# Dense layers in two passes over the blocks, float64 weights converted in two portions, and low parts of the expert weights on VectorE

## The chip, the cores and the metric

The kernel runs on one core of one Trainium2 chip. The metric is the device time of one execution in microseconds; less is better. 787.5 us is the median of three runs (787.34 to 787.77).

## What is computed

Three stages follow each other; `x` of one is the input of the next.

```python
# 1. linear attention: B, H, S, D = 4, 8, 768, 48
cur = einsum('bhd,bhe->bhde', u * k_t, v_t)
y_t = einsum('bhd,bhde->bhe', r_t, state + cur)
state = w * state + einsum('bhd,bhe->bhde', k_t, v_t)
# 2. experts: 3072 tokens of 384, 8 experts of width 1024, top 1
y[mask] = gate_w * (relu(x[mask] @ w1[e]) @ w2[e]);  x = x + y
# 3. dense layers, width 2048
h = x @ w_in
out = (h * tanh(log1p(exp(min(h, 20))))) @ w_out
```

`w_in` and `w_out` arrive in float64. The chip is given their 64-bit words and makes float32 values of them.

## The kernel before

**Numbers in two parts.** Matrix products of stages 2 and 3 run in a 32-bit matmul format that keeps fewer bits than float32. Each operand is held as a high part (a ScalarE copy into that format) and a low part (the operand minus its high part), and a product is three matmuls: high by high, low by high, high by low.

**Attention** (lines 673 to 760): 24 units `u` (6 chunks of 128 tokens by 4 pairs of heads). `load_unit(u + 3)` loads two tiles of a later unit through SP's queue; three buffers hold the `at` tiles, so that a load waits until `cv_unit` (L409) has read the buffer's last content. Per unit VectorE scales (L351, L352), masks (L392, two), adds (L463) and multiplies (L409); GpSimd multiplies twice (L361, L371). Results go to `xd` in memory. Routing into slots of 256 tokens per expert follows.

**Weights.** `wb` holds 32 expert bundles of 128x1536 float32, each with 256 columns of `w1` and the matching rows of `w2`. `bundle_load` (L106) loads one, `bundle_hi` (L118, ScalarE, L121) and `bundle_lo` (L123, L125, VectorE or GpSimd) split it into a ring of five slots. Bundles 0 to 2 are split in quarters during attention (`WU`, L659), their low parts on GpSimd; bundle 3 before the expert loop, the other 28 in the loop, low parts in turn on VectorE and GpSimd (L892). `w64` holds 8 dense bundles of 128x1536 float64. `conv` (L165) turns a piece of 384 columns into float32: a ScalarE absolute value (L178), five VectorE instructions (L180, L183, L187, L189, L191) and a GpSimd addition (L194). There are 32 pieces. Six are done in attention, two steps a unit (`conv_step(2)`, L686), 26 in the expert loop and just ahead of it, two together every second iteration (`conv_most`, L899).

**Experts** (L875 to 900): 32 iterations `i`, one bundle each. TensorE does `gemm1(i + 1)` (18 matmuls of 256 columns, L826) and `gemm2(i)` (12 of 384 columns, L848). VectorE forms the low part of the hidden values (L836), of the next expert's tokens (L810) and the expert's output (L855). The split of bundle `i + 4` and the conversion follow on each engine's queue in the order in which they are written; nothing reorders them.

**Dense layers** (L1194 to 1213): 6 blocks of 512 tokens, block by block, 16 items `f` of 128 hidden columns each: 96 items. `ff1(i + 2)` (9 matmuls of 512 columns, L1101) fills one of four PSUM banks `h`. ScalarE and VectorE turn it into `g` and its two parts (`act_in`, `act_inv`, `act_g`, `act_split`; five VectorE and five ScalarE instructions of 128x512). `ff2(i - 2)` (9 matmuls, L1162) adds into three PSUM banks `o`, which a block's last item empties (L1168 ScalarE twice, L1170 VectorE once). The next block's transposes (L1081 to 1083) lie in items 6, 8 and 10. For the last 16 items `ff1` runs three items ahead instead of two (`LA`). The split of the dense bundles is done at the end of the expert stage and at the start of the dense stage, on VectorE (L911, L1177) and GpSimd (L1178 to 1190, L1212).

Of the kernel before, what the change touches and what calls it, by code (L numbers as in the profile page):

```python
# [34 lines left out]
NLO_A = 2  # L35
HC = 384
W_LO, W_HI = 0.8, 1.25
E20 = 485165195.40979
F64_TINY = 3.4332275390625e-05
# [3 lines left out]
def kernel(  # L43
# [24 lines left out]
    pc = pa.enter_context(tc.tile_pool(name="pc", bufs=1))  # L68
    rs_ = ExitStack()
    ws = rs_.enter_context(tc.tile_pool(name="ws", bufs=3, side="right"))  # L70
    wc_ = rs_.enter_context(tc.tile_pool(name="wc", bufs=2, side="right"))
# [58 lines left out]
    def dense_tile(q, dt=F32):  # L130
        pool = pools["wa"] if q < NLO_A else pools["wb"]
        return pool.tile([128, 1536], dt, tag=f"d{q}", name=f"d{q}")

    def dense_f32(q):
        if q not in dense_t:
            dense_t[q] = dense_tile(q)
        return dense_t[q]

    def dense_hi(q, lo=0, hi=1536):
        n = q + (q > 0)  # L140
        if lo == 0:
            h = ring_tile((NE * NB1 - NW_A - NW_B + n // 2) % (NW_A + NW_B), "hl"[n % 2])
            wtile[NE * NB1 + q] = [h, None]
        A.activation(out=wtile[NE * NB1 + q][0][:, lo:hi], in_=dense_f32(q)[:, lo:hi], func=ACTF.Copy)

    def dense_lo(q, eng, lo=0, hi=1536):
        w = wtile[NE * NB1 + q]
        if lo == 0:
            w[1] = dense_tile(q - 1, F32R) if q else ring_tile((NE * NB1 - NW_A - NW_B) % (NW_A + NW_B), "l")
        eng.tensor_tensor(out=w[1][:, lo:hi], in0=dense_f32(q)[:, lo:hi], in1=w[0].bitcast(F32)[:, lo:hi], op=ALU.subtract)  # L150

    cv_raw = {}

    def conv_load():
# [5 lines left out]
        more = "mp1" in pools and n % 3 == 2  # L160
        t = (pools["mp1"] if more else wc_).tile([128, HC], I64, tag="r64", name="r64")
        nc.sync.dma_start(out=t, in_=w64[q, :, HC * s:HC * s + HC])
        cv_raw[n] = t

    def conv():  # L165

        n = cnt["conv"]
        if n >= NCV:
            return
        cnt["conv"] += 1  # L170
        q, s = divmod(n, NHC)
        if not wide:
            nc.sync.dma_start(out=dense_f32(q)[:, HC * s:HC * s + HC], in_=w64[q, :, HC * s:HC * s + HC])
            return
        raw = cv_raw.pop(n).bitcast(I32).rearrange("p (n two) -> p n two", two=2)
        lo, hi = raw[:, :, 0], raw[:, :, 1]
        mag = wc_.tile([128, HC], F32, tag="mag", name="mag")
        A.activation(out=mag, in_=hi.bitcast(F32), func=ACTF.Abs)  # L178
        a = wc_.tile([128, HC], I32, tag="cva", name="cva")
        V.tensor_scalar(out=a, in0=hi, scalar1=3, scalar2=0x3FFFFFF8,  # L180
                        op0=ALU.logical_shift_left, op1=ALU.bitwise_and)
        yield
        V.scalar_tensor_tensor(out=a, in0=hi, scalar=-0x40000000, in1=a, op0=ALU.bitwise_and, op1=ALU.bitwise_or)  # L183
        yield
        b = wc_.tile([128, HC], F32, tag="cvb", name="cvb")

        V.scalar_tensor_tensor(out=b, in0=mag, scalar=F64_TINY, in1=a.bitcast(F32), op0=ALU.is_ge, op1=ALU.mult)  # L187
        yield
        V.tensor_scalar(out=a, in0=b.bitcast(I32), scalar1=-0x800000, scalar2=None, op0=ALU.bitwise_and)  # L189
        yield  # L190
        V.scalar_tensor_tensor(out=mag, in0=lo.bitcast(U32), scalar=2.0 ** -52, in1=a.bitcast(F32),  # L191
                               op0=ALU.mult, op1=ALU.mult)
        yield
        G.tensor_tensor(out=dense_f32(q)[:, HC * s:HC * s + HC], in0=b, in1=mag, op=ALU.add)  # L194
        yield

    cheld = []

    def conv_most(n):

        new = [conv() for _ in range(n)]
        for c in new:
            next(c, None)
        for _ in range(4):
            for c in new:
                next(c, None)
        cheld.extend(new)

    def conv_sum():
        while cheld:  # L210
            next(cheld.pop(0), None)
# [19 lines left out]
    def load_unit(u):  # L231
        if u >= NU:
            return
        if u == 3:

            a = ws.tile([128, 1536], F32, tag="raw", name="raw")[0:PP].rearrange("p (n b t) -> p n b t", n=3, b=B)
            t = dense_tile(NLO_A - 1)[:, 0:4 * B * D].rearrange("p (n b d) -> p n b d", n=2, b=B)
# [45 lines left out]
    n = 1  # L283
# [375 lines left out]
    WU = [3, 4, 5, 6, 9, 10, 11, 12, 15, 16, 17, 18]  # L659
    cgen = []  # L660

    def conv_step(n):
        for _ in range(n):
            if not cgen and cnt["conv"] < NLO_A * NHC and u >= 3:
                cgen.append(conv())
            if cgen:
                try:
                    next(cgen[0])
                except StopIteration:
                    cgen.pop()  # L670
                    conv_load()

    for u in range(NU):
        c, hp = divmod(u, HP)
        load_unit(u + 3)
        if u == 0:
            bundle_load()
            conv_load()
            conv_load()
        if u in (1, 2) or u - 1 in WU[3::4]:  # L680
            bundle_load()
# [3 lines left out]
        if c != 3 or hp == 0:  # L685
            conv_step(2)  # L686
# [178 lines left out]
    while cgen:  # L865
        conv_step(1)
    bundle_load()
    conv_load()
# [6 lines left out]
    for i in range(NE * NB1):  # L875
        e, p = divmod(i, NB1)
        bundle_load()
        conv_load()
# [400 lines left out]
```

## Time and profile before

| | us |
|---|---|
| median of three runs | 787.5 |
| the profiled execution | 792.44 |
| its span, first to last instruction | 790.7 |
| VectorE busy | 631.5 (80% of the span) |
| TensorE busy | 733.8 (93%) |
| ScalarE busy | 439.9 (56%) |
| GpSimd busy | 218.0 (28%) |

The profile is one execution; it took 4.9 us more than the median. Busy times are averages over three stages: attention and routing end at about 175 us, the experts at about 357 us, and the dense layers run from 367 us to the end. Matmuls overlap one another, so that TensorE's busy share says little; the distance between the starts of matmuls is read instead. An instruction's time includes time in which it has started and cannot proceed.

### The profile page before, as it was taken

Reading aid. Unit: us, or ns where it says so; the run is one execution under the profiler, and the core shown is the slowest. Engines: PE = TensorE matmul, PEld = TensorE weight load, DVE = VectorE, ACT = ScalarE, POOL = GpSimd, SP = SyncE. Lnnn points to the kernel's source line nnn. Section 1 sums busy time; section 2 is a strip of 40 time slices with the busy share of each in tenths; the row PEclk is TensorE's granted clock in tenths of the full one; section 3 lists DMA queues with packets and bytes.
Section 4 is the critical chain, followed back from the end, with each engine's and each line's share of the span. In section 5 each row is a group of like instructions: output and inputs, shape, how many; then the busy total and the mean of one; then the engine's idle time right before and its main releaser. Section 6 shows DMA issues by size and latency. Waiting matters only on the chain.

```text
span 790.7 us, 11718 instructions
## 1 busy us (share of the span) xinstructions
PE 733.8 (93%) x4434; PEld 599.1 (76%) x4434; DVE 631.5 (80%) x1065; ACT 439.9 (56%) x733; POOL 218.0 (28%) x169
## 2 busy tenths in 40 slices
PE   8899989889887888998899999999999999999997
PEld 4577766649887878995688878878877887888786
DVE  7688999967999999955868577857867786784885
ACT  2132222224543443535868677867867786785884
POOL 3554646146486766755110000000000000000000
PEclk9899999999999989899899999999999999999999
DMA  8969677545755665504000100020010001000001
GB/s 253 291 189 299 192 234 236 203 129 187 257 195 194 253 217 178 223 25 135 0 1 1 47 34 0 1 80 0 1 53 28 0 1 41 0 1 30 10 1 40
DMA packets 27507, 84.21 MB, mean 106 GB/s; under 512 B 3481, under 2 KB 9754, under 8 KB 27440
## 3 DMA queue, kind: packets, MB, share of 16 engines
q1 hardware_dynamic: 22512, 73.99, 28.6%
q0 software_dynamic: 2048, 5.44, 2.1%
q10 hardware_dynamic: 2880, 3.93, 1.5%
q8 instruction: 36, 0.59, 0.3%
q14 instruction: 31, 0.25, 0.1%
HBM read 71.63 MB, written 12.58 MB: 106 GB/s over the span
## 4 chain that ended last, share of the span: by engine, by line
PE 49%; DVE 2%; ACT 1%; DMA 1%; issue 0%; SPq 0%
PE o L1162 24%; PE h L1101 24%; PE ptr L1081 1%; DMA xm<-xd 1%; DVE t L1132 1%; DVE g L1134 1%; DVE t L1131 0%; ACT os L1168 0%; DVE gl L1144 0%; ACT e L1110 0%; ACT gh L1143 0%; DVE e L1111 0%; ACT l L1121 0%; SPq L1070 0%; ACT l L1122 0%
## 5 line engine op out<-in xcount | busy, mean ns | idle before, releaser
L1144 DVE TENSOR_TENSOR gl<-g,gh 128x512 fp32r<-128x512 f32 x96 | 66.4, 692 | 27.3 <-ACT gh L1143 26.8
L1143 ACT ACTIVATE gh<-g 128x512 fp32r<-128x512 f32 x96 | 60.7, 633 | 25.9 <-DVE g L1134 25.8
L1162 PE MATMUL o<-gh,d 128*128 128x512 f32 x252 | 74.3, 395 | 0.0
L1101 PE MATMUL h<-xh,d 128*128 128x512 f32 x252 | 73.0, 398 | 0.0
L1121 ACT ACTIVATE l<-s,one 128x512 f32<-128x512 f32 x96 | 69.6, 725 | 3.2
L125 POOL TENSOR_TENSOR wl<-raw,wh 128x1536 fp32r<-128x1536 f32 (+1 forms) x26 | 65.0, 2500 | 17.7 <-ACT wh L121 17.1
L1132 DVE SCALAR_TENSOR_TENSOR t<-t,l 128x512 f32<-128x512 f32 x96 | 66.5, 692 | 3.3
L1134 DVE SCALAR_TENSOR_TENSOR g<-t,h 128x512 f32<-128x512 f32 x96 | 65.9, 687 | 3.3
L1131 DVE SCALAR_TENSOR_TENSOR t<-s,l 128x512 f32<-128x512 f32 x96 | 65.6, 684 | 0.0
L1119 ACT ACTIVATE s<-e 128x512 f32<-128x512 f32 x96 | 59.6, 620 | 7.0 <-DVE e L1111 5.8
L835 ACT ACTIVATE rh<-g 128x512 fp32r<-128x512 f32 x31 | 18.6, 599 | 79.4 <-PE g L826 77.3
L1122 ACT ACTIVATE l<-l 128x512 f32<-128x512 f32 x96 | 60.8, 633 | 3.0
L1110 ACT ACTIVATE e<-h 128x512 f32<-128x512 f32 x96 | 56.0, 583 | 2.1 <-PE h L1101 2.1
L1101 PEld LDWEIGHTS h<-xh,d 128*128 128x128 f32 x252 | 47.7, 189 | 11.7
L1162 PEld LDWEIGHTS o<-gh,d 128*128 128x128 f32 x252 | 47.2, 187 | 11.5
L1111 DVE TENSOR_SCALAR e<-e 128x512 f32<-128x512 f32 x96 | 45.4, 473 | 10.8 <-ACT e L1110 10.5
L1162 PE MATMUL o<-gl,wh 128*128 128x512 f32 x180 | 53.6, 395 | 0.0
L1101 PE MATMUL h<-xh,wh 128*128 128x512 f32 x180 | 52.6, 401 | 0.3 <-DVE g L1134 0.3
L1162 PE MATMUL o<-gh,wh 128*128 128x512 f32 x180 | 52.7, 401 | 0.0
L1101 PE MATMUL h<-xl,wh 128*128 128x512 f32 x180 | 51.7, 395 | 0.0
L826 PE MATMUL g<-xlo,wh 128*128 128x256 f32 x192 | 32.1, 307 | 20.0 <-DVE xlo L810 20.0
L443 ACT ACTIVATE tb<-st 48x192 f32<-48x192 f32 x32 | 11.6, 362 | 68.1 <-DVE st L440 57.3
(218 smaller groups left out, 1735.5 us busy)
## 6 DMA issues: line engine op xcount, KB each, us to landing
raw<-in_wb SPq DMA_DIRECT2D x32, 768.0 KB, 6.8
at<-in_att SPq DMA_DIRECT2D x22, 672.0 KB, 6.2
r<-in_w SPq DMA_DIRECT2D x32, 384.0 KB, 5.4
tk<-in_tok SPq DMA_DIRECT2D x23, 384.0 KB, 5.8
out<-os SPq DMA_DIRECT2D x18, 256.0 KB, 2.2
xd<-xs ACTq DMA_DIRECT2D x20, 192.0 KB, 5.1
xm<-xd SPq DMA_DIRECT2D x5, 768.0 KB, 4.8
xd<-xs SPq DMA_DIRECT2D x4, 192.0 KB, 1.9
```

Of the source, the lines that this page charges most:

```text
L125: eng.tensor_tensor(out=l[:, lo:hi], in0=raw_t[i][:, lo:hi], in1=h.bitcast(F32)[:, lo:hi], op=ALU.subtract)
L1101: T.matmul(ps, lhsT=w_[:, c0:c0 + 128], rhs=x_[:, k, :], start=(n + k == 0), stop=(n + k == KD + 1))
L1110: A.activation(out=e, in_=h_p[i], func=ACTF.Exp)
L1119: A.activation(out=s, in_=s_t[i], func=ACTF.Square)
L1121: A.activation(out=l, in_=s, func=ACTF.Ln, bias=one)
L1122: A.activation(out=l, in_=l, func=ACTF.Exp, scale=-1.0)
L1131: V.scalar_tensor_tensor(out=t, in0=s_t.pop(i), scalar=1.0, in1=r, op0=ALU.add, op1=ALU.mult)
L1132: V.scalar_tensor_tensor(out=t, in0=t, scalar=-2.0, in1=r, op0=ALU.add, op1=ALU.mult)
L1134: V.scalar_tensor_tensor(out=g, in0=t, scalar=0.5, in1=h_p.pop(i), op0=ALU.add, op1=ALU.mult)
L1143: A.activation(out=gh, in_=g, func=ACTF.Copy)
L1144: V.tensor_tensor(out=gl, in0=g, in1=gh.bitcast(F32), op=ALU.subtract)
L1162: T.matmul(oacc[bk][k], lhsT=w_[:, c0:c0 + 128], rhs=g_, start=(f == 0 and n == 0), stop=(f == NF - 1 and n == 2))
```

## The change

- The dense layers go over the blocks twice. First columns 0 to 1023 of `w_in` (items 0 to 7) for blocks 0 to 5; block 5 goes straight on with items 8 to 15, and then blocks 4 to 0 do items 8 to 15. The split input of blocks 0 to 3 is stored in memory (`xd_t`) and loaded again; those of blocks 4 and 5 stay. Half sums of blocks 0 to 4 are stored in `od`, loaded again, and added by VectorE when the second half is done.
- Dense bundles 0 to 3 are converted in the expert loop, none in attention; bundles 4 to 7 beside the first half of the dense layers. A piece has 768 columns (16 pieces). It takes an absolute value (ScalarE), a maximum with a constant (GpSimd), five VectorE instructions, the last of which is the addition that GpSimd did. One VectorE instruction is queued per step: one or two steps per expert iteration, one per dense item.
- All low parts of the bundles in the expert loop, and all of the dense bundles, are made by VectorE.
- Loads: expert bundles are loaded at units 3, 7, 13, 15, 18 and 21, not 0, 1, 2, 7, 13 and 19; two pieces of `w64` at units 22 and 23. The quarters of bundles 0 to 2 are split two units later.
- `ff1` runs three items ahead from item 40 on.

```diff
-HC = 384
+HC = 768
+NB_B = 4
...
+    def dense_home(q, part):
+        if q < 2:
+            return pools["wb"].tile([128, 1536], F32R, tag=f"e{'hl'[part]}{q}", name=f"e{'hl'[part]}{q}")
+        if q < NB2 - 1:
+            return ring_tile(q % (NW_A + NW_B), "hl"[part])
+        return dense_tile(part, F32R)
...
+    def conv_mag(n):
+        if n in mag_t or n not in cv_raw:
+            return
+        mag_t[n] = wc_.tile([128, HC], F32, tag="mag", name="mag")
+        A.activation(out=mag_t[n], in_=cv_raw[n][:, :, 1].bitcast(F32), func=ACTF.Abs)
+        G.tensor_scalar(out=mag_t[n], in0=mag_t[n], scalar1=F64_TINY, scalar2=None, op0=ALU.max)
...
+            conv_mag(n)
+            yield
...
+            V.tensor_scalar(out=a, in0=a, scalar1=3, scalar2=0x3FFFFFF8,
+                            op0=ALU.logical_shift_left, op1=ALU.bitwise_and)
+            yield
+            V.scalar_tensor_tensor(out=a, in0=hi, scalar=-0x40000000, in1=a, op0=ALU.bitwise_and, op1=ALU.bitwise_or)
+            yield
+            V.tensor_scalar(out=b.bitcast(I32), in0=a, scalar1=-0x800000, scalar2=None, op0=ALU.bitwise_and)
+            yield
+            V.scalar_tensor_tensor(out=b, in0=lo.bitcast(U32), scalar=2.0 ** -52, in1=b, op0=ALU.mult, op1=ALU.mult)
+            cv_raw.pop(n)
+            conv_load()
+            yield
+            V.tensor_tensor(out=d, in0=a.bitcast(F32), in1=b, op=ALU.add)
+            conv_mag(n + 1)
+        if q < 2 or q >= NB_B:
+            dense_hi(q, lo_, hi_)
+            yield
+            dense_lo(q, lo_, hi_)
         yield
...
-        if u == 0:
+        if u in (3, 7, 13, 15, 18, 21):
             bundle_load()
+        if u in (22, 23):
             conv_load()
-            conv_load()
-        if u in (1, 2) or u - 1 in WU[3::4]:
-            bundle_load()
...
-        if c != 3 or hp == 0:
-            conv_step(2)
...
-            bundle_lo(j, G if i % 2 else V)
-        elif j == NE * NB1:
-            dense_hi(0)
-            dense_lo(0, V)
+            bundle_lo(j, V)
...
-        if i % 2:
-            conv_most(2)
+        conv_step(1 + (i % 4 > 0), NB_B * NHC)
...
-    for q in range(1, 6):
-        dense_hi(q)
-        if q == 2:
-            dense_lo(1, V)
+    conv_step(99, NB_B * NHC)
+    dense_hi(2)
     expert_y(NE - 1, 1)
     scatter(NE - 1, 1)
+    dense_lo(2)
+    dense_hi(3)
+    dense_lo(3)
...
+    NFH = 2 * NB_B
+    items = [(bk, f) for bk in range(NBLK) for f in range(NFH)] + \
+            [(bk, f) for bk in reversed(range(NBLK)) for f in range(NFH, NF)]
...
+    def x_keep(bk):
+        if bk < NBLK - 2:
+            for p in range(2):
+                nc.sync.dma_start(out=xd_t[bk, p], in_=xT_b[bk][p].bitcast(F32).rearrange("p k t -> p (k t)"))
+
+    def x_again(bk):
+        if 0 <= bk < NBLK - 2:
+            x_tiles(bk, bk % 2)
+            for p in range(2):
+                nc.sync.dma_start(out=xT_b[bk][p].bitcast(F32).rearrange("p k t -> p (k t)"), in_=xd_t[bk, p])
...
-    LA = NI - 16
+    LA = NBLK * NFH - NFH
...
+            if f > 0:
+                for k in range(KD):
+                    o_t[k] = f1.tile([128, 512], F32, tag=f"os{k}", name="os")
+                    nc.sync.dma_start(out=o_t[k], in_=od[bk, k])
...
+                if f == NF - 1 and bk < NBLK - 1:
+                    o = o_t[k]
+                    V.scalar_tensor_tensor(out=o, in0=oacc[bk][k], scalar=2.0, in1=o, op0=ALU.mult, op1=ALU.add)
...
-    for q in range(2, 4):
-        dense_lo(q, V)
-    dense_lo(4, G)
...
-    dense_lo(5, G)
-    dense_hi(6)
-    dense_lo(6, G)
+    conv_step(7)
...
         act_g(i - 1)
+        conv_step(1)
...
-        if i < NI and f in (6, 8, 10):
-            block_x(bk + 1, (f - 6) // 2)
+        if f in (1, 3, 5):
+            block_x(bk + 1, f // 2)
...
+        if i + 4 < NI and items[i + 3][1] == NF - 1:
+            x_again(items[i + 3][0] - 2)
```

## Rows read from the trace of the kernel before

**Rows 1.** Busy time by stretch: length, PE, PEld, DVE, ACT, POOL, clock, DMA share, GB/s.

```profile
0.00:165.00 165.00, 148.47 (x1571) 106.79 (x1572) 143.13 (x318) 44.26 (x109) 76.22 (x88) 0.96 0.77 232
175.00:353.00 178.00, 153.35 (x981) 150.09 (x980) 164.47 (x208) 79.00 (x103) 118.97 (x66) 0.91 0.55 194
353.00:384.00 31.00, 23.86 (x96) 17.24 (x95) 17.80 (x19) 19.00 (x25) 12.59 (x6) 0.86 0.27 90
455.55:524.57 69.02, 68.75 (x301) 55.09 (x301) 51.03 (x85) 51.03 (x86) 0.00 (x0) 1.00 0.07 24
```

**Rows 2.** The chain of waits, in the dense layers: start, length, engine, tile, line.

```profile
457.90 2.10 PE o L1162 x9
460.00 2.10 PE h L1101 x9
```

**Rows 3.** Timeline of VectorE and GpSimd in the expert loop: start, length, instruction.

```profile
248.23 4.13 DVE L180 TENSOR_SCALAR cva<-r 128x384 int32<-128x384 int32 x2
...
259.70 4.12 DVE L180 TENSOR_SCALAR cva<-r 128x384 int32<-128x384 int32 x1
...
248.60 3.53 POOL L125 TENSOR_TENSOR wl<-raw,wh 128x1536 fp32r<-128x1536 f32 x1
```

**Rows 4.** Busy time of the conversion's VectorE instructions (tile cva), before and from 173.

```profile
0.00:173.00 173.00, 18.42 (x30) 0.96 0.75 226
173.00:353.00 180.00, 101.74 (x130) 0.91 0.55 195
```

**Rows 5.** Instructions by line: shortest, median and longest in ns.

```profile
L180 DVE TENSOR_SCALAR cva<-r x32: 341/352/4132, 31.7 to 333.5; 128x384 int32<-128x384 int32 x32
L183 DVE SCALAR_TENSOR_TENSOR cva<-r,cva x32: 536/546/3861, 32.1 to 334.3; 128x384 int32<-128x384 int32 x32
L125 POOL TENSOR_TENSOR wl<-raw,wh x26: 1002/3498/4377, 38.5 to 341.7; 128x1536 fp32r<-128x1536 f32 x14, 128x384 fp32r<-128x384 f32 x12
L125 DVE TENSOR_TENSOR wl<-raw,wh x15: 1736/1895/2037, 177.4 to 338.7; 128x1536 fp32r<-128x1536 f32 x15
```

**Rows 6.** Timeline of TensorE in one expert iteration that waits for nothing.

```profile
184.49 0.87 PE L826 MATMUL g<-xhi,wh 128*128 128x256 f32 x6
...
186.64 0.86 PE L848 MATMUL acc<-wh,rh 128*128 128x384 f32 x4
...
188.73 0.82 PE L807 MATMUL ptr<-ident,xg 128*128 128x128 f32 x6
```

**Rows 7.** Who waited for whom, VectorE: us in total, times, longest.

```profile
DVE os L1170 <- PE o L1162: 34.2, 6, 8.1
...
DVE kp L351 <- DMA at<-in_att: 13.0, 8, 4.0
```

**Rows 8.** Costliest groups of the page: busy us, mean ns; dense layers.

```profile
L1144 DVE TENSOR_TENSOR gl<-g,gh 128x512 fp32r<-128x512 f32 x96 | 66.4, 692 | 27.3 <-ACT gh L1143 26.8
```

**Rows 9.** ScalarE groups by shape: busy us, mean ns of one.

```profile
L121 ACT ACTIVATE wh<-raw 128x1536 fp32r<-128x1536 f32 x29 | 43.1, 1485 | 0.0
...
L178 ACT ACTIVATE mag<-r 128x384 f32<-128x384 f32 x32 | 17.1, 558 | 17.4 <-POOL d L194 11.4 <-DMA r<-in_w 3.9 <-ACT xs L476 2.2
```

**Rows 10.** Timeline at the start of the dense layers: GpSimd, VectorE, TensorE.

```profile
370.11 3.50 POOL L150 TENSOR_TENSOR d<-d,wh 128x1536 fp32r<-128x1536 f32 x1
370.81 3.09 DVE L1111 TENSOR_SCALAR e<-e 128x512 f32<-128x512 f32 x1 [1.89 <-ACT e L1110]
...
379.64 1.65 PE L1101 MATMUL h<-xh,wl 128*128 128x512 f32 x3 [3.20 <-DVE g L1134]
```

**Rows 11.** Timeline of VectorE in the dense layers behind a block's end: one item.

```profile
455.41 0.42 DVE L1111 TENSOR_SCALAR e<-e 128x512 f32<-128x512 f32 x1
...
458.85 0.42 DVE L1111 TENSOR_SCALAR e<-e 128x512 f32<-128x512 f32 x1
```

**Rows 12.** DMA issues of the page: KB each, median us from issue to landing.

```profile
raw<-in_wb SPq DMA_DIRECT2D x32, 768.0 KB, 6.8
```

More of the change, by code (lines that the diff above doesn't have):

```diff
@@ L159, in conv_load @@
         q, s = divmod(n, NHC)
-        more = "mp1" in pools and n % 3 == 2
-        t = (pools["mp1"] if more else wc_).tile([128, HC], I64, tag="r64", name="r64")
+        t = wc_.tile([128, HC], I64, tag=f"r64{n % 2}", name="r64")
         nc.sync.dma_start(out=t, in_=w64[q, :, HC * s:HC * s + HC])
-        cv_raw[n] = t
+        cv_raw[n] = t.bitcast(I32).rearrange("p (n two) -> p n two", two=2)
+    def conv_mag(n):
[4 more added lines that the diff above has]
+        G.tensor_scalar(out=mag_t[n], in0=mag_t[n], scalar1=F64_TINY, scalar2=None, op0=ALU.max)
@@ L165, in conv @@
     def conv():
         n = cnt["conv"]
-        if n >= NCV:
-            return
         cnt["conv"] += 1
         q, s = divmod(n, NHC)
+        lo_, hi_ = HC * s, HC * s + HC
+        d = dense_f32(q)[:, lo_:hi_]
         if not wide:
[L173 to L177, printed above, removed]
@@ L188, in conv @@
[L188 to L207, printed above, removed]
@@ L209, in conv_sum @@
-    def conv_sum():
-        while cheld:
-            next(cheld.pop(0), None)
+            nc.sync.dma_start(out=d, in_=w64[q, :, lo_:hi_])
+        else:
+            conv_mag(n)
+            yield
+            raw = cv_raw[n]
+            lo, hi = raw[:, :, 0], raw[:, :, 1]
+            a = mag_t.pop(n).bitcast(I32)
+            b = wc_.tile([128, HC], F32, tag="cvb", name="cvb")
+            V.tensor_scalar(out=a, in0=a, scalar1=3, scalar2=0x3FFFFFF8,
[11 more added lines that the diff above has]
+            conv_mag(n + 1)
@@ L214, with conv_step @@
+        if q < 2 or q >= NB_B:
+            dense_hi(q, lo_, hi_)
+            yield
+            dense_lo(q, lo_, hi_)
+        yield
+    cgen = []
+    def conv_step(n, upto=NCV):
+        for _ in range(n):
+            if not cgen and cnt["conv"] < upto:
+                cgen.append(conv())
+            if cgen:
+                try:
+                    next(cgen[0])
+                except StopIteration:
+                    cgen.pop()
     slots = rt.tile([128, 2, 2, NE, 3], BF16, name="slots")
@@ L658 @@
     RT = {3: (0, 12), 4: (12, 4), 5: (16, 4)}
[L659 to L670, printed above, removed]
-                    conv_load()
+    WU = [5, 6, 7, 8, 11, 12, 13, 14, 17, 18, 19, 20]
     for u in range(NU):
@@ L877 @@
         bundle_load()
-        conv_load()
         if p == 2:
@@ L1076, in block_x @@
         if k == 0:
-            xT_b[bk] = [f2.tile([128, KD, 512], F32R, tag=f"x{n}", name=f"x{n}") for n in "hl"]
+            x_tiles(bk, bk % 2)
         hi, lo = xT_b[bk]
@@ L1091, in ff1 @@
             return
-        bk, f = divmod(i, NF)
+        bk, f = items[i]
         q, s = divmod(f, 2)
@@ L1149, in ff2 @@
             return
-        bk, f = divmod(i, NF)
+        bk, f = items[i]
         q, s = divmod(f, 2)
         wh, wl = wtile[NE * NB1 + q]
-        if f == 0:
+        first_ = f == 0 or (f == NFH and bk < NBLK - 1)
+        last_ = f == NF - 1 or (f == NFH - 1 and bk < NBLK - 1)
+        if first_:
             oacc[bk] = [psO.tile([128, 512], F32, tag=f"o{k}", name=f"o{k}") for k in range(KD)]
+            if f > 0:
+                for k in range(KD):
+                    o_t[k] = f1.tile([128, 512], F32, tag=f"os{k}", name="os")
+                    nc.sync.dma_start(out=o_t[k], in_=od[bk, k])
         gh, gl = gs_t.pop(i)
         parts = ((wh, gh), (wl, gh), (wh, gl))
-        for n, k in [(0, k) for k in range(KD)] + ([(n, k) for k in range(KD) for n in (1, 2)] if f == NF - 1 else
+        for n, k in [(0, k) for k in range(KD)] + ([(n, k) for k in range(KD) for n in (1, 2)] if last_ else
                                                    [(n, k) for n in (1, 2) for k in range(KD)]):
@@ L1175 @@
     keep_warm(10)
-    for q in range(2, 4):
-        dense_lo(q, V)
-    dense_lo(4, G)
-    xT_b[0] = [f2.tile([128, KD, 512], F32R, tag=f"x{n}", name=f"x{n}") for n in "hl"]
+    x_tiles(0, 0)
     first = [psO.tile([128, 512], F32, tag=f"o{k}", name="ptr") for k in range(KD)]
@@ L1194 @@
     for i in range(NI + 2):
-        bk, f = divmod(i, NF)
+        bk, f = items[min(i, NI - 1)]
         act_in(i)
```

77 lines of the change are left out of this document (31 added, 46 removed).

## The prediction

> **What bounds the kernel now.** I read the busy times by stretch first, to find what limits each stage; then the chain of waits, which only reaches back to the start of the dense layers; then, for the expert stage, the timeline and the length of single instructions.
>
> In the dense layers TensorE is the limit. The chain there is nothing but matmuls, 2.10 us for each nine [rows 2], so that an item takes 4.20, and a block takes 69.02 [rows 1], of which 16 items are 67.2. The other 1.8 are twelve transposes and a block's end. VectorE is busy for 51.0 of the 69.0 and has room.
>
> In the expert stage VectorE is the limit: 164.5 busy of 178, while TensorE, which would need less, is kept waiting. The reader is to see why it is so busy. Two conversion instructions that take 0.352 each by their median [rows 5] last 4.13 together, and they start just ahead of a GpSimd subtraction of 3.53 and end behind it [rows 3]. Eleven and a half us later the same happens again; this is one turn of two iterations. The 130 conversion instructions of this stage are busy for 101.7 [rows 4]. At their medians a piece takes 2 x 0.352 + 3 x 0.546 = 2.34 (the three of its five instructions that have no row are of these two kinds), and 26 pieces 60.9. So 41 us of VectorE's time here is standing beside GpSimd.
>
> In attention nothing is full: VectorE 143.1 of 165, DMA engines 0.77 of 165, that is 127 [rows 1]. VectorE waits 13.0 for the `at` loads [rows 7].
>
> **The change, part by part.** The sum is made against the profiled execution (792.4); it is 4.9 above the median, and I take the same differences off the median. A change within 0.2% (1.6 us) couldn't be told from none.
>
> *Attention.* Six pieces go, 18.4 of VectorE's time [rows 4]. VectorE's floor becomes 143.1 - 18.4 = 124.7. The DMA floor stays near 127: the units' tiles are the same, and fewer pieces of `w64` only just count. If VectorE keeps its 21.9 of idle time, the stage takes 146.6: **-18**. Loading the first expert bundles later takes them out of the crowded first 50 us and could give back most of the 13.0 as well: -27 at best. If the DMA engines, which are then wanted for 127 of 147, can't be kept busy over 0.80 of the time, the stage takes 159: -6. I take -18, the row of VectorE's work, since both floors lie well under it. The quarters of bundles 0 to 2 are the same instructions two units later: nothing. The two loads at units 22 and 23 come behind the last unit's tiles on SP's queue: nothing; with no cover one landing of 6.8 [rows 12].
>
> *Expert stage, VectorE.* Of the 164.5, 101.7 were conversion and 15 x 1.895 = 28.4 low parts [rows 5]; the remaining 34.4 stay. Now 29 low parts of 1.74 (the shortest; no subtraction on GpSimd is left to stand beside) are 50.5. For a piece of 768 columns there is no row. A one-input instruction takes 0.352 for 384 columns [rows 5] and 0.42 for 512 [rows 11], so about 0.56; a two-input one 0.546, 0.692 [rows 8] and 1.74 for 384, 512 and 1536, so about 0.96. A piece is 2 x 0.56 + 3 x 0.96 = 4.0, eight are 32.0, and four low parts of bundles 0 and 1 are 3.8. Sum: 120.7. Two costs come on top. The maximum on GpSimd has no row; its nearest is the subtraction, 1.00 for 384 and 3.50 for 1536 columns [rows 5], so from nothing to 1.83 per piece; I take half, 0.9, as it has one input, 7 for eight. And ScalarE's absolute value for the next piece is queued behind this piece's addition, ahead of the next iteration's hidden values: 0.87 between 0.558 and 1.485 [rows 9], with a high part of the same length behind it for two bundles: twelve times 0.87, 10, in which VectorE's next instruction may wait. Together 138.
>
> The Trainium skill, "Perfetto Trace Analysis", section "Optimizing Scalar/DVE Operations", says that work may be given to GpSimd where VectorE is saturated, and warns that the two share a read port. Its first half speaks against this change, by which the stage would gain nothing (a rival below); rows 3 and 5 bear out the warning.
>
> *Expert stage, TensorE.* An iteration that waits for nothing takes 188.73 - 184.49 = 4.24, with six transposes of 0.82 behind it for each expert [rows 6]: 32 x 4.24 + 8 x 0.82 = 142.2. Both engines now want about 140. They run in written order and wait on each other in each iteration, so I add 7% to the larger: 152, **-26**. Bounds: TensorE's floor and 3 for its slow first matmuls, -33; VectorE with the dearest maximum (145.7) and one 128x512 instruction's time lost in each of 32 iterations (22), 168, -10. Conversion loads now stand on SP's queue between bundle loads and wait for a VectorE step; a bundle is asked for three iterations ahead (13 us) and lands in 6.8, so nothing.
>
> *Start of the dense layers.* Three GpSimd subtractions go from there. Now one makes the first item's VectorE instruction take 3.09 instead of 0.42, TensorE then waits 3.20, and it comes back slowly, three matmuls in 1.65 [rows 10]; the granted clock of the stretch is 0.86 [rows 1]. That is some 7 with the slow matmuls. In exchange seven steps, 4.0 + 0.96 of VectorE, stand ahead of the first item; four PSUM banks let TensorE go on for 8.4 meanwhile. **-4**, from -7 to +3.
>
> *Block ends.* There are ten inside the stage in place of five. The five new ones lie in the second half, where TensorE is three items ahead, and a wait of part of the 1.8 above is mostly covered; all three sums are on VectorE, 3 x 0.69, where an item takes VectorE 3.44 [rows 11] against 4.20. **+1**, from 0 to +4. Stores and loads of the split input (768 KB) and of half sums are read four items (17 us) or more after their issue, against 6.8 to land, and the DMA share of a block is 0.07: nothing; uncovered, 6.8 each. Behind them on SP's queue wait only loads of the same kind and the outputs.
>
> *First half of the dense layers.* This is the price. Eight items take TensorE 8 x 4.20 + 1.8 = 35.4. VectorE's 51.0 for 16 items hold four instructions of a block's end and transposes, 2.5, so an item is 3.03; eight are 24.3, and 2.5 for the ends, as there are as many per eight items now. A piece and its low part add 5.0: 31.8. With 0.9 beside the maximum, and 1.7 while ScalarE does an absolute value and a high part ahead of the next item, 34.4. That is 97% of TensorE's time. TensorE has an item in hand, so I let half of the last two, 1.3, come through in each of 57 / 8 = 7.1 pieces: **+9**. Bounds: 0, if the idle time takes it all; +25, if 3.6 of each 7.6 come through.
>
> Sum: -18 - 26 - 4 + 1 + 9 = -38. The profiled execution would come to 754.4, the median to 749.5.
>
> **The rivals.**
>
> 1. *As worked out*: 749.5, own range 738 to 762. Chance 0.55.
> 2. *VectorE becomes the bound of the first half.* For: 97%, and waits on ScalarE in a fixed order. Against: an item's slack, and VectorE's wait of 34.2 at six block ends [rows 7], which shows that it runs ahead now. First half +25: 765.5. Chance 0.17.
> 3. *Both stages come near their floors*: attention -24, experts -33, start -6, first half +2, ends +1: 727.5. For: nothing is full any more. Against: order of the queues. Chance 0.12.
> 4. *Attention is held by its loads*, -6 in place of -18: 761.5. For: the DMA floor of 127. Chance 0.06.
> 5. *GpSimd's part was free*: the 41 us come from elsewhere, and conversion instructions stay as long. Then VectorE has 101.7 x 16 / 26 + 8 x 0.96 + 29 x 1.9 + 34.4 + 3.8 = 164, as before; the expert stage gains nothing: 775.5. It is what the skill's page would give without its warning. Rows 3 speak against it. Chance 0.03.
> 6. *Slower: the conversion is not hidden in the dense layers at all.* In the queue's order each step falls between `g` and the next item's first instruction, and TensorE is full there now, so what isn't hidden is paid whole. Price 7.1 x 7.6 = 54, against 47 gained elsewhere: 794.5. It turns slower when more than 47 of the 54 comes through. Against: VectorE is idle for 18 in 69 now. Chance 0.07.
>
> **How the numbers follow.** The predicted time is that of the first case, 749.5. The range 729 to 777 takes in cases 2, 4 and 5 and half of case 3; outside are case 6, the other half of 3 and the tails, about 0.18. Faster by over 0.2%: cases 1 to 5 less their tails, 0.89. Within 0.2%: 0.03, between cases 5 and 6. Slower: 0.08.
>
> **What would show it right or wrong.** The last matmul of the experts some 44 us earlier; no VectorE instruction of the conversion over 1.5 us in that stage, and no wait of GpSimd's length; the units of attention 0.8 us shorter each, and not more than 13 us of waits for `at`. In the dense layers: second-half blocks of about 34.5 each, first-half blocks of 36 to 37, with TensorE's waits ending on `g` or on `gl`. If the first half shows VectorE busy all the time, case 2 or 6 holds; if attention ends later than 155 with waits for loads, case 4.

## The result, and the profile after

The changed kernel takes 757.83 us (median, 754.35 to 758.23) against 787.42 for the kernel before in the same series: a ratio of 0.9623, interval 0.9586 to 0.966. The forecast was 749.5 in a range of 729 to 777, with a chance of 0.89 that it would be faster.

Of the page after, the busy times [for before: the table ahead of the prediction]:

```profile
span 755.9 us, 11683 instructions
PE 717.5 (95%) x4428; PEld 582.8 (77%) x4434; DVE 603.6 (80%) x1024; ACT 440.2 (58%) x720; POOL 145.0 (19%) x132
```

Busy time by stretch of the kernel after, beside [rows 1]: attention, to 10 us ahead of the experts as there; the experts from their first matmul to the end of their last; the stretch from there to the first dense matmul; two blocks' first halves; one second half in mid-stage; the last second half.

```profile
core 0: us, PE busy (x) PEld busy (x) DVE busy (x) ACT busy (x) POOL busy (x), PEclk, DMA share, GB/s
0.00:150.00 150.00, 140.85 (x1554) 103.49 (x1559) 125.36 (x286) 40.47 (x102) 67.93 (x83) 0.95 0.79 244
160.20:305.80 145.60, 142.78 (x1002) 140.12 (x1002) 118.58 (x136) 74.36 (x88) 51.01 (x34) 1.00 0.62 210
305.80:319.85 14.05, 6.60 (x25) 3.69 (x26) 4.61 (x5) 4.29 (x5) 5.70 (x4) 0.75 0.43 138
371.83:407.81 35.98, 35.40 (x157) 28.02 (x156) 31.00 (x51) 28.88 (x47) 2.27 (x1) 1.00 0.32 110
407.81:443.81 36.00, 35.43 (x157) 28.03 (x156) 31.02 (x51) 28.89 (x47) 2.28 (x1) 1.00 0.32 110
621.10:654.79 33.69, 33.69 (x145) 26.91 (x144) 25.93 (x43) 24.07 (x40) 0.00 (x0) 1.00 0.26 94
722.17:750.59 28.42, 24.27 (x100) 18.17 (x99) 23.27 (x39) 18.24 (x30) 0.00 (x0) 1.00 0.17 56
```

The reader is to see TensorE busy in 142.78 of the experts' 145.60: in this stage it has taken VectorE's place as the limit. The same stretches of the profile before and of three executions that change one thing (the experts from their first matmul to the end of their last; "to dense" from there to the first dense matmul; "dense start" from that to the first matmul of the second layer; "dense in all" to the last instruction):

| | experts begin | experts | to dense | dense start | dense in all | span |
|---|---|---|---|---|---|---|
| before | 175.0 | 182.4 | 9.7 | 16.6 | 423.7 | 790.7 |
| after | 160.2 | 145.6 | 14.0 | 18.6 | 436.1 | 755.9 |
| before, low parts on VectorE | 167.9 | 154.6 | 8.9 | 16.6 | 423.7 | 755.1 |
| after, low parts in turn | 158.9 | 165.1 | 14.1 | 18.5 | 435.2 | 773.3 |
| after, no dense conversion | 159.3 | 148.2 | 11.9 | 12.4 | 424.7 | 744.1 |

So 14.8 and 36.8 were gained in the first two stages, and 4.3 and 12.4 given back: 34.8 of span in all. TensorE's matmuls of the expert stage are busy for 142.8 us at a granted clock of 1.00; before they were busy for 157.6 at 0.91. Instructions of the conversion after, shortest, median and longest in ns, where [rows 3, 5] had pairs of 4.13 us:

```profile
L173 POOL TENSOR_SCALAR mag<-mag x16: 2129/2181/2901, 168.2 to 541.1; 128x768 f32<-128x768 f32 x16
L191 DVE TENSOR_SCALAR mag<-mag x16: 550/553/559, 173.3 to 556.3; 128x768 int32<-128x768 int32 x16
L194 DVE SCALAR_TENSOR_TENSOR mag<-r,mag x16: 950/953/959, 173.9 to 559.8; 128x768 int32<-128x768 int32 x16
L125 DVE TENSOR_TENSOR wl<-raw,wh x29: 1744/1758/1761, 162.2 to 290.1; 128x1536 fp32r<-128x1536 f32 x29
```

None of VectorE's is stretched any more.

### The profile page after: what moved, and what is told of

It reads as the page before. It is cut to its first block, busy times and chain, and to the rows that moved or that the text cites. A ratio compares the mean times of both kernels' runs of the same rounds, so it can differ in the third digit from the quotient of the medians.

```text
span 755.9 us, 11683 instructions
## 1 busy us (share of the span) xinstructions
PE 717.5 (95%) x4428; PEld 582.8 (77%) x4434; DVE 603.6 (80%) x1024; ACT 440.2 (58%) x720; POOL 145.0 (19%) x132
## 4 chain that ended last, share of the span: by engine, by line
PE 40%; DVE 12%; ACT 5%; issue 1%; DVEq 0%; ACTq 0%
PE h L1108 21%; PE o L1176 19%; DVE t L1139 2%; DVE g L1141 2%; DVE gl L1151 2%; DVE t L1138 2%; ACT gh L1150 1%; PE ptr L1087 1%; ACT e L1117 1%; DVE d L202 1%; ACT mag L172 1%; ACT wh L149 1%; DVE e L1118 1%; ACT os L1185 0%; DVE xl L1089 0%
## 5 line engine op out<-in xcount | busy, mean ns | idle before, releaser
L173 POOL TENSOR_SCALAR mag<-mag 128x768 f32<-128x768 f32 x16 | 35.8, 2239 | 242.9 <-ACT mag L172 242.9
L1126 ACT ACTIVATE s<-e 128x512 f32<-128x512 f32 x96 | 60.1, 626 | 37.3 <-DVE e L1118 36.4
L1118 DVE TENSOR_SCALAR e<-e 128x512 f32<-128x512 f32 x96 | 40.9, 426 | 22.5 <-ACT e L1117 22.5
L125 DVE TENSOR_TENSOR wl<-raw,wh 128x1536 fp32r<-128x1536 f32 x29 | 50.9, 1754 | 7.1 <-ACT wh L121 6.5
L1176 PE MATMUL o<-gh,wl 128*128 128x512 f32 x180 | 53.3, 395 | 0.0
L1108 PE MATMUL h<-xh,wl 128*128 128x512 f32 x180 | 52.4, 399 | 0.0
L121 ACT ACTIVATE wh<-raw 128x1536 fp32r<-128x1536 f32 (+1 forms) x41 | 49.4, 1204 | 0.6 <-ACT xs L485 0.4
L1108 PEld LDWEIGHTS h<-xh,wh 128*128 128x128 f32 x180 | 33.6, 190 | 15.5 <-DVE g L1141 7.9
L828 ACT ACTIVATE rh<-g 128x512 fp32r<-128x512 f32 x31 | 18.5, 598 | 40.8 <-PE g L819 38.3
```

The source lines that it names most:

```text
L125: eng.tensor_tensor(out=l[:, lo:hi], in0=raw_t[i][:, lo:hi], in1=h.bitcast(F32)[:, lo:hi], op=ALU.subtract)
L1108: T.matmul(ps, lhsT=w_[:, c0:c0 + 128], rhs=x_[:, k, :], start=(n + k == 0), stop=(n + k == KD + 1))
L1126: A.activation(out=s, in_=s_t[i], func=ACTF.Square)
L1176: T.matmul(oacc[bk][k], lhsT=w_[:, c0:c0 + 128], rhs=g_, start=(first_ and n == 0), stop=(last_ and n == 2))
```

## The experiments

**1. The kernel before, once more** (no edit), to see how far two executions of one kernel differ.

> The kernel before, profiled once more, to see which stage made its first profiled execution (792.4) 4.9 us longer than the median (787.5). Theory: the expert stage, where TensorE waits and its granted clock was 0.91; the first to last expert matmul takes 177 to 178 in place of 182 us, with a higher granted clock, and attention and the dense layers are within 0.5 us of the first profile. Rival: attention, whose loads run at 0.77 of the DMA engines; then the first expert matmul starts 4 to 5 us earlier than 175.0 and the expert stage keeps its 182.

It took 788.5 us. The experts begin at 172.3, and last 183.0: the theory, which put the difference into the expert stage, missed; of the 3.9 us between the two profiled executions 2.7 lie ahead of the experts. A third execution with the same attention code (next) has 167.9. The first stage alone varies by 7 us.

**2. Low parts, each way round.** In the kernel before, all on VectorE; in the changed kernel, in turn on GpSimd again.

```diff
-            bundle_lo(j, G if i % 2 else V)
+            bundle_lo(j, V)
```

> The kernel before with one part of the change alone: all low parts of the bundles in the expert loop on VectorE. Theory (VectorE's long instructions stand beside GpSimd's subtraction of 3.5 us): of each turn of two iterations, 11.5 us, 3.5 of standing go and 1.75 of work come; 13 turns with a conversion give 1.7 each, so the expert stage is some 20 us shorter, the time 767 (762 to 775), and no conversion instruction lasts over 2.5 us. Rival (GpSimd's part was free for VectorE): 14 x 1.75 = 24.5 us more of VectorE's time, 812.

> The changed kernel with the low parts of the expert bundles in turn on VectorE and GpSimd again. Theory (they make VectorE stand): per turn 1.75 us of VectorE's work go and up to 3.5 of standing come, so VectorE needs 8 + 1.75 = 9.7 or more against TensorE's 8.9 to 9.1; the expert stage, 145 us in the changed kernel, becomes 155 to 170 and the time 767 to 782. Rival (GpSimd is free, and the gain came from converting half as much there): the stage stays at 145, bound by TensorE, 757 to 759.

They took 758.97 (ratio 0.962, 0.9587 to 0.9653) and 775.64 (0.978, 0.9714 to 0.9847; four executions from 768.49 to 781.71). This one line gives the kernel before as much as the whole change gives; the time is 8 us below its theory's 767. Its undoing costs the changed kernel 12 by the ratios and 18 by the medians. One kind of conversion instruction in the expert stage of the kernel before, and the same with this line changed:

```profile
L180 DVE TENSOR_SCALAR cva<-r 128x384 int32<-128x384 int32 x26 | 43.4, 1709 | 0.0
```

```profile
L180 DVE TENSOR_SCALAR cva<-r 128x384 int32<-128x384 int32 x26 | 8.0, 350 | 0.0
```

The five kinds together fall from 105.7 to 56.0, 49.7 less, for some 25 us of low parts that VectorE does in addition. TensorE gains too: its matmuls of the stage are busy for 145.0 at a granted clock of 0.99, in place of 157.6 at 0.91. The experts of the changed kernel with low parts in turn, by stretch; two GpSimd subtractions with a VectorE instruction beside each; and one group:

```profile
158.90:324.00 165.10, 150.60 (x1002) 147.52 (x1002) 130.34 (x122) 74.18 (x88) 100.30 (x48) 0.95 0.55 186
```

```profile
227.33 3.51 POOL L125 TENSOR_TENSOR wl<-raw,wh 128x1536 fp32r<-128x1536 f32 x1 [4.28 <-ACT wh L121]
227.37 4.28 DVE L198 SCALAR_TENSOR_TENSOR cvb<-r,cvb 128x768 f32<-128x768 uint32 x1
...
239.83 3.52 POOL L125 TENSOR_TENSOR wl<-raw,wh 128x1536 fp32r<-128x1536 f32 x1 [0.82 <-ACT wh L121]
...
240.84 0.68 DVE L829 SCALAR_TENSOR_TENSOR rl<-g,rh 128x512 fp32r<-128x512 f32 x1
```

```profile
L198 DVE SCALAR_TENSOR_TENSOR cvb<-r,cvb 128x768 f32<-128x768 uint32 x8 | 21.1, 2634 | 0.1
```

The conversion step that takes 0.95 alone lasts 4.28: it starts with the GpSimd subtraction of 3.51 and ends 0.81 behind it. In the mean the step takes 2.63. Taking 14 low parts from VectorE (20.2 us less in the group of L125) costs it 30.6 in the five groups of the conversion (62.3 against 31.7, 40 instructions each). The hidden values' low part (L829, one of its two inputs in PSUM) is not touched: 0.68 in the midst of the second subtraction, and 0.68 to 0.69 in all 31. The Trainium skill, "SBUF — State Buffer", section "Who interferes with whom", says that only the pair of ports which VectorE and GpSimd share causes contention, as an exclusive lock, and that a VectorE instruction with at most one SBUF input, outside the modes that use both ports, is free of it. The rows agree with both.

**3. Attention.** The kernel before without conversion in attention (all in the expert loop); and the changed kernel with its bundle loads at the units of before.

```diff
-        if c != 3 or hp == 0:
-            conv_step(2)
...
+    conv_sum()
```

```diff
-        if u in (3, 7, 13, 15, 18, 21):
+        if u in (0, 1, 2, 7, 13, 19):
             bundle_load()
```

> The kernel before without conversion in attention; its six pieces are done in the expert loop, where they make three more turns. Theory (VectorE's 18.4 us of conversion set attention's length): the first expert matmul starts at 161 to 163 in place of 175.0; three turns of 11.5 in place of about 8.9 add 8; time 782 (779 to 786). Rival (the loads set it, and the change shortened attention by moving the first bundle loads): the first expert matmul stays at 171 to 175, and the time is 792 to 796.

> The changed kernel with its expert bundles loaded at units 0, 1, 2, 7, 13 and 19, as in the kernel before. Theory: attention got shorter by the conversion that left VectorE, as the kernel before without conversion in attention has it (first expert matmul at 163.5 against 167.9 to 175.0); the later loads gave the 3 us beside it or nothing: first expert matmul at 160 to 164, time 757 to 761. Rival: the loads' crowding of the first 50 us was half of it: first expert matmul at 165 to 168, waits for the attention tiles 13 us or more against 10.7, time 762 to 766.

The first: 793.43 (1.0057, 1.0034 to 1.008); its theory's 782 missed. The experts begin at 163.5, some 8 sooner than the mean of the three with the conversion there, but last 192.8, 10 longer, and the stretch to the dense stage is 14.2 where it was 9.7. Six pieces moved from attention into a stage that VectorE limits gave nothing in all. Not all of the 10 is the pieces: 3 to 5 are lost in the first five iterations, where ScalarE once waits 6.03 for something that the profile does not name.

The second took 789.99 (0.9999, 0.9969 to 1.003). Both theories missed. The experts begin at 190.0, 30 later, and all stages behind stay as they were (experts 145.1, dense 434.8). What SP's queue waited for in attention, in us, times, longest; first of this run, then of the changed kernel:

```profile
SPq L254 <- DVE cv L418: 62.8, 13, 11.1
SPq L112 <- POOL wl L125: 36.0, 3, 13.7
```

```profile
SPq L254 <- DVE cv L418: 74.0, 18, 7.4
...
SPq L112 <- POOL wl L125: 4.2, 1, 4.2
```

The fourth to sixth bundle (units 7, 13, 19) want a `raw` buffer that GpSimd's quarters free, and the changed kernel splits those two units later. The load waits 36.0 on SP's queue, and the tiles of attention wait behind it. So later loads and later quarters are one edit; my run undid half of it, and what the placement is worth by itself stays open. The prediction had costed the quarters at nothing, which holds only because the loads went with them.

**4. The maximum on VectorE**, in place of GpSimd.

```diff
-        G.tensor_scalar(out=mag_t[n], in0=mag_t[n], scalar1=F64_TINY, scalar2=None, op0=ALU.max)
...
+            V.tensor_scalar(out=mag_t[n], in0=mag_t[n], scalar1=F64_TINY, scalar2=None, op0=ALU.max)
             a = mag_t.pop(n).bitcast(I32)
```

> The changed kernel with the maximum of each piece on VectorE instead of GpSimd. The trace after has the maximum at 2.18 us on GpSimd, 16 times. Theory: VectorE has room in the expert stage and almost in the dense layers; 0.56 us of work comes where up to 1.7 of standing goes, so nothing that can be measured: 756 to 759, expert stage 144 to 146. Rival (each maximum holds VectorE up by some 1.6 us on the path): 8 x 1.6 in each of two stages, 735 to 745.

It took 765.1 (0.969, 0.9651 to 0.9729): slower than the changed kernel by 5 to 7, against both theories. The experts took 8.4 more (154.0; the profiles that leave the expert loop as it is have 145.1 to 148.2), with VectorE busy in 123.1 of them. Most of this is not the price of eight maxima of 0.553. ScalarE stands twice at the start of the stage, for something that the profile does not name:

```profile
167.27 0.60 ACT L828 ACTIVATE rh<-g 128x512 fp32r<-128x512 f32 x1 [5.07 <-remote]
174.38 0.60 ACT L828 ACTIVATE rh<-g 128x512 fp32r<-128x512 f32 x1 [6.51 <-remote]
```

The fifth of these copies starts 24.4 into the stage instead of 18.5; from there to the end it is 129.5 instead of 127.0. Why the start is lost was not settled, and so it is not shown that GpSimd is the better place for the maximum itself.

**5. The conversion in the dense stage taken away.**

```diff
-    NCV = NB2 * NHC
+    NCV = NB_B * NHC
...
-    conv_step(7)
+    for q in range(NB_B, NB2):
+        wtile[NE * NB1 + q] = wtile[NE * NB1 + q - NB_B]
```

> The changed kernel without the conversion beside the dense layers. It leaves out pieces 8 to 15 (dense bundles 4 to 7); items 8 to 15 use bundles 0 to 3 in their place, as many matmuls of the same shape. Theory: conversion there is mostly hidden, as the trace after shows half-blocks of 36.0 us against 35.4 for TensorE; some 4 us of waits in the first half and 4 in the start of the dense layers (seven steps ahead of the first item) go; 750 (747 to 753). Rival (the prediction's price, 9 in the first half): 745 or less, half-blocks under 35.2. Rival 2 (the waits are those of block ends, not of the conversion): half-blocks stay at 36.0, 754.

It took 747.49 (0.9472, 0.9422 to 0.9522). The dense stage is 11.4 shorter: 6.2 of it at the start (12.4 instead of 18.6) and 5.2 behind. A first half by stretch, beside the 36.00 above:

```profile
399.83:435.26 35.43, 35.15 (x157) 28.10 (x156) 26.89 (x45) 26.95 (x45) 0.00 (x0) 1.00 0.25 89
```

A piece and its low part cost TensorE 0.57 per eight items, 4.0 for seven: VectorE's 4.1 more per eight items fit into its idle time almost wholly.

**6. The start of the dense stage.** The changed kernel's start, where seven steps stand ahead of the first item's `e`:

```profile
321.63 0.55 DVE L191 TENSOR_SCALAR mag<-mag 128x768 int32<-128x768 int32 x1
...
327.46 0.96 DVE L153 TENSOR_TENSOR wl<-d,wh 128x768 fp32r<-128x768 f32 x1 [1.71 <-ACT wh L149]
328.34 0.86 DVE L1118 TENSOR_SCALAR e<-e 128x512 f32<-128x512 f32 x1
...
334.40 1.65 PE L1108 MATMUL h<-xh,wh 128*128 128x512 f32 x3 [3.92 <-DVE g L1141]
```

First edit: the last pieces and low parts behind the last expert's output, and no steps ahead of the first item (two in every eighth instead). Second edit: two steps in each iteration of the expert loop, three in two of them. Third: as the second, and the first five steps of the ninth piece in the expert loop too.

```diff
-    conv_step(99, NB_B * NHC)
-    dense_hi(2)
     expert_y(NE - 1, 1)
     scatter(NE - 1, 1)
-    dense_lo(2)
+    conv_step(99, NB_B * NHC)
+    dense_hi(2)
     dense_hi(3)
-    dense_lo(3)
...
-    conv_step(7)
...
-        conv_step(1)
+        if i < 2:
+            dense_lo(2 + i)
+        conv_step(1 + (i % 8 == 7))
```

```diff
-        conv_step(1 + (i % 4 > 0), NB_B * NHC)
+        conv_step(2 + (i % 16 == 4), NB_B * NHC)
```

```diff
-        conv_step(1 + (i % 4 > 0), NB_B * NHC)
+        if i < 29:
+            conv_step(2 + (i % 4 == 0 and i < 28), NB_B * NHC + 1)
...
-    conv_step(99, NB_B * NHC)
...
-    conv_step(7)
+    conv_step(2)
```

> The changed kernel with the work around the branch between experts and dense layers in another order: the last expert's output and scatter ahead of the conversion's remaining steps, the low parts of dense bundles 2 and 3 in the first two dense items, the seven conversion steps ahead of the first item spread over later items. Theory (TensorE waits because VectorE and GpSimd come late to the branch, and then because VectorE converts a piece ahead of the first item): from the last expert matmul to the first of the dense layers 9 to 10 us in place of 13 to 14; from there to the first matmul into o 14 to 15 in place of 18.5; time 750 (748 to 753). Rival (the gap is the loads of block 0's input, which wait for the scatter before): gap unchanged, time 754 to 758.

> The changed kernel with two conversion steps in every iteration of the expert loop (three in two of them), so that all eight pieces are done by iteration 28 and no maximum stands on GpSimd behind that. Theory: the 14.0 us from the last expert matmul to the first dense one (before: 9.7) come from a maximum in iteration 29, behind which GpSimd's scatter of expert 6 stands; the later scatters and the loads of the first block's tokens follow in a chain. Then this stretch falls to 9.5 to 11, the expert stage becomes 145.5 to 148, and the time 754 (751 to 757). Rival: the branch and the low parts of the dense bundles set it; then the stretch stays at 13 to 15 and the time at 757 to 760.

> As the kernel with the steps earlier, and the first five steps of the ninth piece are made in the expert loop too, so that two steps instead of seven stand ahead of the first dense item. Theory: the 18.6 us from the first dense matmul to the first of the second layer are 12 to 13 plus these VectorE steps; here 12 to 13.5, nothing is lost later since the pieces stay in step with the half blocks (36.0 each), and VectorE's 3 us more in the expert stage cost 0 to 3; 748.5 (745 to 752). Rival: what the start gains is lost again before the first half ends, as where the low parts were put behind the start (6.7 gained there, 2.4 left): 752 to 756.

| | time (range) | ratio | experts | to dense | dense start | dense in all |
|---|---|---|---|---|---|---|
| first | 760.27 (757.1 to 761.63) | 0.9624, 0.9579 to 0.9668 | 147.1 | 14.3 | 11.9 | 433.7 |
| second | 756.65 (754.59 to 759.34) | 0.9592, 0.9545 to 0.9639 | 149.5 | 8.9 | 18.2 | 434.8 |
| third | 755.77 (749.52 to 759.79) | 0.9544, 0.9491 to 0.9596 | 155.5 | 9.2 | 13.6 | 430.0 |

By their ratios none of the three can be told from the changed kernel (0.9586 to 0.966); the first and third missed their theories' times (750 and 748.5). In the traces the places named gave what they were asked for, but for the stretch to the dense stage in the first, and none of the runs kept it all. The first won 6.7 at the start, and lost 4.3 behind: its first halves take 36.4, 37.4 and 38.0 where they took 36.0. That with nine steps to eight items the pieces no longer keep step with the blocks is my reading, and was not tried. In the second the stretch to the dense stage fell by 5.1, but the experts grew by 3.9; TensorE's waits in them are 6.3 where they were 2.3. Here are GpSimd's instructions at this end in the changed kernel and in the second:

```profile
299.69 2.13 POOL L173 TENSOR_SCALAR mag<-mag 128x768 f32<-128x768 f32 x1 [3.93 <-ACT mag L172]
302.00 1.35 POOL L855 DMA_INDIRECT xd<-xm,sid  x1 [0.18 <-issue]
307.01 0.99 POOL L855 DMA_INDIRECT xd<-xm,sid  x1 [3.65 <-DVE xm L848]
308.01 2.17 POOL L173 TENSOR_SCALAR mag<-mag 128x768 f32<-128x768 f32 x1
310.65 2.45 POOL L855 DMA_INDIRECT xd<-xm,sid  x1 [0.47 <-DVE wl L153]
319.58 0.09 POOL L1055 MEMSET one<- 128x1 f32 x1 [6.48 <-PE wp L270]
```

```profile
307.04 0.99 POOL L855 DMA_INDIRECT xd<-xm,sid  x1 [2.24 <-DMA xd<-xm,sid]
310.37 1.41 POOL L855 DMA_INDIRECT xd<-xm,sid  x1 [2.34 <-DMA xd<-xm,sid]
317.45 0.10 POOL L1055 MEMSET one<- 128x1 f32 x1 [5.67 <-PE wp L270]
```

The maximum at 299.69 stands ahead of the first of these scatters, and the others follow one after the other. Counted from the end of the last expert matmul (305.67 and 308.61), the last scatter starts 5.0 behind in the changed kernel and 1.8 in the second. It is 4.8 to 5.2 in the six profiles with a maximum in this place, and 1.8 to 2.2 in the four without, experiment 4's among them. In both kernels the memset, which needs no data, runs 5.7 to 6.5 behind that scatter, with the first dense matmul 0.3 later; before it was 5.8 as well (359.71 + 0.98 to 366.47); over all profiles it is 5.2 to 8.5, which blurs differences of this stretch by some 3 us. Between them each engine reads a flag and jumps past the part for rare inputs. What takes the six us there was not tried. The profile's DMA view has 8 packets that load instructions in the 14.2 us from 305.7 to 319.9, and 7 in the 100 us from 200 to 300; whether an engine stands for them is not shown.

The third shows why steps can't be moved into the expert loop for nothing. VectorE is busy in only 122.1 of its 155.5 us; the loss begins on ScalarE's queue:

```profile
199.03 0.96 DVE L202 TENSOR_TENSOR d<-mag,cvb 128x768 f32<-128x768 f32 x1
200.02 0.89 ACT L172 ACTIVATE mag<-r 128x768 f32<-128x768 f32 x1 [6.07 <-DVE d L202]
200.81 0.83 ACT L149 ACTIVATE eh<-d 128x768 fp32r<-128x768 f32 x1
201.54 0.85 ACT L802 ACTIVATE xhi<-ptr 128x512 fp32r<-128x512 f32 x2
202.18 1.65 PE L819 MATMUL g<-xhi,wh 128*128 128x256 f32 x6 [3.33 <-ACT xhi L802]
```

The next piece's absolute value waits 6.07 for VectorE's addition, the next expert's tokens (`xhi`) stand behind it, and TensorE waits for these 3.33. Its waits for `xhi` are 6.8 in four places, where the changed kernel has one of 0.2. The granted clock of the stage is 0.97 instead of 1.00, mostly the upper of its two levels, 2.4 GHz, and its matmuls, as many, are busy for 147.2 instead of 142.8. Longer waits (5.9 more in all) and slower matmuls (4.4) make up the some 10 us by which the stage is longer.

**7. Half sums one item later**, alone, and then with the third edit of 6.

```diff
-            for k in range(KD):
-                if f == NF - 1 and bk < NBLK - 1:
...
+            if f == NF - 1 and 0 < bk < NBLK - 1:
+                held.append(bk)
+            else:
+                outputs(bk, f)
...
+        while held:
+            outputs(held.pop(), NF - 1)
         ff2(i - 2)
```

> The changed kernel with the sums at a second-half block's end (three VectorE instructions that wait for TensorE's last matmuls) queued one item later on VectorE, behind the next item's instructions. Theory (at the last block end VectorE stands 4.3 us for TensorE, and the eight items behind it run at VectorE's and ScalarE's 3.5 us an item, TensorE waiting 5.3 in all): the last half-block takes 25 to 26 us in place of 28.4, the others stay at 33.7; time 754.5. Rival (the next block's first matmul into o then waits for the sums): half-blocks of 34.5 or more, no gain.

> The steps earlier, five of them ahead of the dense stage, and the half sums' additions one item later as in the run that did this alone (3.5 us of that run's gain lay in the last half block, 24.9 instead of 28.4). Theory: the three gains lie in three places and add up: 744.5 (741 to 749), expert stage 146 to 149, stretch to the dense stage 9.5 to 11, its start 12 to 13.5, last half block 25. Rival: they share one slack and do not add: 749 to 753.

Alone it took 754.25 (752.02 to 756.92), 0.9555 (0.9511 to 0.9598), an interval that just meets the change's own. Its last half block by stretch, beside 28.42 above:

```profile
724.74:749.64 24.90, 23.63 (x100) 18.40 (x99) 20.26 (x33) 15.24 (x25) 0.00 (x0) 1.00 0.19 64
```

That is 3.5 of the 4.9 by which its dense stage is shorter, as its theory had it; the half blocks in mid-stage are 33.60 instead of 33.69. Together they took 753.01 (749.11 to 755.52), 0.9534 (0.9494 to 0.9574), experts 155.2, dense 426.2. This beats both kernels, and its interval lies just under the change's own (0.9586 to 0.966); from the run with the sums alone it can't be told. The gains did not add up to the theory's 744.5: the dense stage gained 9.9, and the experts paid 9.6; what is left is the stretch between them, some 4.5 shorter.

## Why the prediction was right, point by point

| term | forecast | found |
|---|---|---|
| attention | -18 (-27 to -6) | -14.8; means of executions -11.5 |
| experts | 178 to 152, -26 (-33 to -10) | 182.4 to 145.6, -36.8 |
| start of the dense layers | -4 (-7 to +3) | +6.3 (4.3 to dense, 2.0 in it) |
| block ends | +1 (0 to +4) | +5.5, in the last eight items |
| first half of the dense layers | +9 (0 to +25) | +5.2 |

The five found come to -34.6 with the first of the two values for attention, beside 34.8 of span. The means are of the three executions with the conversion in attention (171.7) and of nine with the changed attention (158.9 to 163.4, mean 160.2).

- **The mechanism held.** VectorE's 41 us beside GpSimd were the price, and the low parts give them back. The five kinds of conversion instruction cost 31.7 in the stage, forecast 32.0; low parts 50.9, forecast 50.5. Rival 5, by which GpSimd's part was free, is refuted by experiment 2 in both directions.
- **Experts**: the forecast 152 covers all 32 iterations, but I took it off 178, the stretch to 353, and the stage lasts to 357.4. This is 4.4 of the 10.8 by which the gain is larger, and why it lies beyond the bound of -33. The other 6.4 is the 7% that I added for two engines waiting on each other, which was too much. TensorE waits 2.3 in the whole stage, so it came out at the floor of the bounds (142.2 and 3). The 10 for ScalarE's absolute value isn't paid as the change places its steps; the wait named there is real, as the third edit of 6 shows.
- **Start of the dense layers**: this step failed, and came out beyond its bound. Without the seven steps the start takes 12.4 (experiment 5), 4.2 less than before, where I gave some 7 to the subtractions; the steps cost 6.2. I costed seven steps of 5.0 as covered by TensorE's four banks. With what ScalarE does in between they hold the first `e` until 328.34, 8.5 behind the first matmul; the banks are then full, and TensorE waits 3.92 and comes back with 1.65 for three matmuls, the same price that I let vanish with the GpSimd subtractions [rows 10]. And I did not look at what stands on GpSimd's queue ahead of the last scatters: the maxima of the conversion, some 3 of the 4.3 ahead of the dense layers by experiment 6.
- **First half**: forecast 36 to 37 per half block, found 36.0; without conversion 35.4, as forecast. Case 2 (VectorE the bound) and case 6 (nothing hidden) are both out, since 0.57 of each 4.1 (31.0 less 26.9 of VectorE per eight items) comes through.
- **Block ends**: covered all through the second half, as argued, but for the last, and there beyond the bound of 4. From the first matmul into `o` of the last eight items to the last instruction it was 25.4 (765.36 to 790.72) and is 30.9 (725.00 to 755.91), 5.5 more. Before, these items still came every 2.1 once no `ff1` followed: VectorE's part was ready. Now the three sums use up that lead, and the items go by VectorE and ScalarE at 3.50. With the sums one item later it is 27.4, so 3.5 of the 5.5 is the sums; the other 2.0 was not tried.
- **Attention**: within bounds, and short of the value taken. VectorE's work came out as costed (125.4, forecast 124.7), but its idle time, which I kept at 21.9, is 24.6 in a shorter stage; of it the waits for `at` are 10.7, before 13.0. By the means of executions the gain lies halfway to that of case 4, which is so not refuted by its size; its sign, a stage of more than 155 with longer waits for loads, did not show (150).
- **The level**: I worked the sum out from a profiled execution that was 4.9 above the median, and took it off the median all the same. The forecast for the profiled execution was 754.4, and it took 757.98: 3.6 off. For the median it was 749.5 against 757.83, since the 4.9 excess of before's profile has no counterpart after. That the sum came so near is in part luck: its misses (experts 10.8 better, start 10.3 worse, block ends 4.5 worse) cancelled for the most part.

## What to carry to other kernels

Before work is given to GpSimd to relieve VectorE, look at what VectorE's two-input instructions take beside it: here the relief cost more than it took (30.6 for 20.2), and one line was worth as much as the whole change. Once an engine in a stage isn't the limit, a moved step is paid by its place in the in-order queues (what is behind it, and what it waits for), not by its length. A load moved on a queue must be checked against the step that frees its buffer: half of such a move cost 30 us.

## What the runs showed of the hardware that was not expected

- The one-input maximum of 128x768 takes GpSimd 2.13 to 2.90 us, 2.8 ns a column by its median, over the bound of 1.83 that I had from a two-input subtraction (3.50 for 1536, 2.3 ns a column); spans of GpSimd are rough in the profile. VectorE takes 0.553 for a one-input instruction of that size. The Trainium skill, "GPSIMD Engine Reference", section 4.1, "Engine selection", says that GpSimd is about half as fast as VectorE in two-input operations, and in one-input ones roughly at line rate. The first agrees with 3.50 against 1.75 for 128x1536; no run here agrees with the second.
- Executions of the same attention code end up to 7 us apart, while a block in the midst of the dense layers repeats within 0.04 (69.01 to 69.05 in three executions).
